# A one-core attention and feed-forward kernel: first steps reordered, state tokens in three passes, second block's low parts and final stores moved

## The chip, the core and the metric

The kernel runs on one core of a Trainium2 chip. The metric is device time in microseconds (us), the median of several executions. Five engines work side by side, each through its own queue in order: TensorE (PE in the profile; its weight loads are PEld), VectorE (DVE), ScalarE (ACT), GpSimd (POOL) and SyncE (SP), which here only issues DMAs. ACT can issue DMAs too. A matmul multiplies a stationary operand (`lhsT`) by a moving operand of up to 512 columns and adds the result up in PSUM.

## The reference

For 8 batches of 512 tokens (`x`) and 32 state tokens (`state`), 8 heads of 64 columns each:

```python
a      = softmax(x @ state^T / 8);  xread = a @ state        # x reads the state
a2     = softmax(state @ x^T / 8);  sread = a2 @ x           # the state reads x
y      = concat(xread, sread)                # 8 x 544 tokens x 512 columns
yn     = (y - mean(y)) / sqrt(var(y) + 1e-6) * g_ln
x2     = y + relu(yn @ w_ch1) @ w_ch2        # feed-forward, 512 -> 2048 -> 512
gate   = sigmoid(causal 5-tap convolution of x2 along the tokens, per column)
out    = (gate * (x2 @ w_val)) @ w_out
```

Inputs `x` and `state` are float32, the weights arrive in 64-bit form and are decoded on the chip.

## The kernel before, in words

**Number formats.** A plain f32 matmul shows as two MATMUL instructions in the profile. Most products use three passes of the faster f32r form instead: each operand is split into a high part (rounded to f32r, by ACT) and a low part (the rest, by a subtraction on DVE or POOL), and `mm3` (L76) issues high times low, low times high, high times high. `split_sb` (L72) makes the two parts.

**Weights.** `w_ch1` and `w_ch2` are 16 tiles each of 128 x 512 (512 KB raw). `tile_stages` (L484) decodes one tile: `decode_a` (two ACT operations), `decode_b` (four DVE operations, L455, L457, L458, L462), and for most `w_ch2` tiles a split. The raw tiles of `w_ch1` share four buffers (`raw`), so the load of tile 4 waits until tile 0 is decoded. The order in which tiles are taken is the list `order` (L730): `w_ch2` tiles 0 and 1, `w_ch1` tile 4, and so on. `share` (L895) says how many are emitted at each block.

**Feed-forward.** Hidden units go in 16 blocks of 128 (`f`), four blocks to a quarter `q`. For ordinary tokens layer 1 is not done on the tokens: `m_steps` (L132) multiplies the 32 state rows of each head by the quarter's weights, `colsum` (L152) supplies the column sums that subtract the mean, and a block is then `h = m^T aT` with `aT` the attention weights. In the first segment (batch 0, `f` 0 to 3) `m`, `aT` and `w_ch2` are plain f32 (L559, L595); all else is three-pass with `ahl`, the split of `aT`. `colsum(q)` for `q` > 0 is four pairs of matmuls into `parts`, an ACT copy (L161), one product over the copy (L163) and another copy.

`segment` (L536) runs the blocks: at each `f` the PE gets `h(f)`, then the second layer of `f - 1` (12 matmuls into four accumulators), and one step of a background generator `bg`. Segments: batch 0 blocks 0 to 7, batch 1 blocks 0 to 7, batch 0 and 1 blocks 8 to 15, batches 2 to 7 whole, and last all 256 state tokens together (`b == B`). For these, layer 1 is the plain product `w1^T xn` of L565, four pairs of 256-column matmuls a block, then ReLU (L580, ACT), its low part (L582, DVE) and layer 2.

**First steps.** Before segment 0 the program lists by hand what PE, ACT and DVE do (L863 to L887): state coefficients, decode of `w_ch1` tiles 0 to 3 (`st`), the scores of batch 0, its softmax, the column sums of quarter 0, `m` of quarter 0, and the decode of `w_ch2` tile 0 (`w20`). `fill` puts warm-up matmuls into PE's queue. `first()` (L779) is the background of segment 0: x1 of batch 0 in two groups, its mean and variance, the attention of batch 1, and the state read of batch 0.

**Second block.** After the state segment, each batch `i` is loaded back from DRAM (`x2d`, into one of two `big` buffers), split (`split_x2`, L637: ACT high, POOL low, for batch 0 DVE low), gated (`gate_x2`, L649: ACT, four DVE taps L658, ACT sigmoid L670), multiplied by `w_val` (`val_steps`, L681) and by `w_out` (`out_steps`, L697). The split and gate of batch 0 and the decode of `w_out` are background of the state segment; those of batch 1 come beside `val_steps(0)`. `w_out`'s raw tiles are loaded into the buffers of `w_ch1` tiles once those are free.

**What sets the order.** Only PE's queue (and in the first steps ACT's and DVE's) follows the program. For the other engines a planner places each operation by priority (`at_prio`; a smaller number goes first, `HLEAD` = 4000 is four blocks ahead) on its own estimated clock, and each engine then keeps that order. `behind(ins, mark)` forbids an operation from being placed ahead of the last one that set the mark (`"dve"`, `"act"`, `"q1"`, `"s"`). Loads go to SP's queue in the planned order; `load_state(0)` and `load_x(0)` go to ACT's.

**Final stores.** The state tokens' output rows are stored as two DMAs of 256 KB (L709), each 4 batches x 32 rows.

Of the kernel before, what the change touches and what calls it, by code (L numbers as in the profile page):

```python
# [9 lines left out]
F32 = mybir.dt.float32  # L10
# [34 lines left out]
def tile_kernel(ctx: ExitStack, tc: tile.TileContext, xT, xk, stT, sn, w1, w2, wval, wout, convw, gln, ident, out):  # L45
# [105 lines left out]

    def colsum(q, between=lambda k: None):  # L152
        if q:
            parts = at_ps([P, S])
            for k in range(KT):
                nc.tensor.matmul(
                    parts[32 * k:32 * k + 32, :], lhsT=g_sb[:, k].to_broadcast([P, 32]), rhs=w1s[4 * q + k],
                    start=True, stop=True,
                )
            t = t2([P, S])  # L160
            nc.scalar.copy(t, parts)  # L161
            cp = at_ps([P, S])
            nc.tensor.matmul(cp, lhsT=part.to_broadcast([P, P]), rhs=t, start=True, stop=True)  # L163
            nc.scalar.copy(cs[:, q], cp)
            cs_done.add(q)
            return
        cp = at_ps([P, S])
        for k in range(KT):
            nc.tensor.matmul(
                cp, lhsT=g_sb[:, k].to_broadcast([P, P]), rhs=w1s[4 * q + k], start=k == 0, stop=k == KT - 1  # L170
            )
            between(k)
        marks["act"] = nc.scalar.copy(cs[:, q], cp)
        cs_done.add(q)
# [39 lines left out]
    def softmax1_split(b):  # L214
        ahls[b] = ahl = sb([P, 2, 2, S], F32R, "ahl")
        for u in range(2):
            split_sb(ahl[:, u, 0], ahl[:, u, 1], aTs[b][:, u], nc.vector)

# [115 lines left out]
    def x1_steps(b):  # L334
        _, sn_raw, _, sbhl = coef[b]
        ahl, aT = ahls[b], aTs[b]
# [12 lines left out]
        mu = at_ps([P, S])  # L349
        for u in range(2):  # L350
            h, l = sbhl[:, 0, u].to_broadcast([P, P]), sbhl[:, 1, u].to_broadcast([P, P])
            mm3(mu, h, l, ahl[:, u, 0], ahl[:, u, 1], u == 0, u == 1)
        sqs = []
        for k in range(KT):
            xc = t2([P, S])
            nc.vector.tensor_tensor(xc, x1[:, k], mu, op=ALU.add)
            nc.scalar.activation(xc, xc, AF.Square)
# [48 lines left out]
    def sread_block_steps():  # L406
# [7 lines left out]
        xc = sb([P, KT, NTS], F32, "big")  # L414
        xn = sb([P, KT, NTS], F32, "ahl")
        for k in range(KT):
            nc.vector.tensor_tensor(xc[:, k], xs[:, k], mu, op=ALU.add)
        yield
        for k in range(KT):
            nc.scalar.activation(xn[:, k], xc[:, k], AF.Copy, scale=g_sb[:, k])  # L420
        xns[B] = xn
# [25 lines left out]
    def decode_a(r, c):  # L447
        a = nc.scalar.activation(c, r[:, :, 1].bitcast(F32), AF.Abs)
        behind(a, "act")
        a = nc.scalar.activation(r[:, :, 0].bitcast(I32), r[:, :, 0], AF.Copy, scale=2.0 ** -29)  # L450
        behind(a, "act")

    def decode_b(r, c):
# [30 lines left out]
    def tile_stages(kind, j):  # L484
        if kind == "1":
# [5 lines left out]
            def second():  # L491
                a = decode_b(r, c)
                if j == 2 * KT - 1:
                    marks["q1"] = a

            return lambda: decode_a(r, c), second, lambda: None
        if kind == "s":
# [9 lines left out]
            return split, lambda: None, lambda: None  # L507
        if j < QF:
            if j % 2 == 0:
# [3 lines left out]
            return lambda: decode_a(r, c), lambda: decode_b(r, c), lambda: None  # L513
        r, c = raws["2", j], sb([P, DM], F32, "c")
# [18 lines left out]
    cs_done = set()  # L533
    clock = [BASE]

    def segment(b, f0, f1, n, nxt, bg):  # L536
        accs = {}
        for f in range(f0, f1):
# [7 lines left out]
            fresh = b < B and unit is not None and unit[1] not in cs_done  # L546
            if b < B and unit is not None and f % QF == 1 and not fresh:
                at_prio(base - 1500)
                m_steps(*unit)
            at_prio(base - HLEAD)  # L550
            if f == 1 and 1 < b < B:
                x1_group(b)
            at_prio(base)
            h = ps(ps_mm, "mm", [P, n])
            if b < B:
                m = ms[b, q]
                for u in range(2):
# [4 lines left out]
                    mm3(h, m[:, u, 0, cols], m[:, u, 1, cols], ahl[:, u, 0], ahl[:, u, 1], u == 0, u == 1)  # L562
            else:
                for k in range(KT):
                    nc.tensor.matmul(  # L565
                        h, lhsT=w1s[4 * q + k][:, cols], rhs=xns[b][:, k], start=k == 0, stop=k == KT - 1
                    )
            if fresh and f % QF == 3:
                at_prio(base - 1500)
                colsum(unit[1])  # L570
                m_steps(*unit)
# [65 lines left out]
    def split_x2(i, k):  # L637
# [4 lines left out]
        behind(nc.scalar.activation(hi, src, AF.Copy), "act")  # L642
        if i:
            nc.gpsimd.tensor_tensor(lo, src, hi.bitcast(F32), op=ALU.subtract)  # L644
# [27 lines left out]
    def x2_steps(i):  # L672
        if i > B:
            return
        for k in range(KT):
            split_x2(i, k)
            yield
            gate_x2(i, k)
            yield

    def val_steps(i):  # L681
# [4 lines left out]
        for e in range(KT):  # L686
# [5 lines left out]
            hl = sb([P, 2, n], F32R, f"w2_{8 + 4 * (i % 2) + e}")  # L692
            split_sb(hl[:, 0], hl[:, 1], gt[:, e], nc.vector)
            gvs[i].append(hl)
            yield

    def out_steps(i):  # L697
        n = ntok(i)
        hls = gvs.pop(i)
        for t in range(n // P):  # L700
# [7 lines left out]
            if i == B:  # L708
                nc.sync.dma_start(out=out[4 * t:4 * t + 4, S:, :], in_=ob[:, t % 2])  # L709
            elif t % 2:  # L710
# [31 lines left out]
    load_state(0, nc.scalar)  # L742
    load_x(0, nc.scalar)
    load_tile("1", 1)
    nc.sync.dma_start(out=g_sb.rearrange("p k o -> p (k o)"), in_=gln)
    for j in range(2, KT):
# [32 lines left out]
    def first():  # L779
# [4 lines left out]
        state_coefs(1)  # L784
        yield
        next(x1)
        yield
# [5 lines left out]
        yield  # L793
        next(att1)
        yield
        for _ in x1:
            pass
        softmax2_turn(0)
        yield
        sread(0)  # L800
# [62 lines left out]
    with tc.manual_schedule(engines={mybir.EngineType.PE, mybir.EngineType.Activation, mybir.EngineType.DVE}):  # L863
# [21 lines left out]
        fill(6)  # L885
        w20[1]()
        slots[0] = decode_slots(order[1:])  # L887
    with tc.manual_schedule(engines={mybir.EngineType.PE}):
# [3 lines left out]
        next(slots[0])  # L892
        at_prio(BASE - 5000)
        softmax1_split(0)
        share[0] = iter([1, 2, 2, 5, 2, 1, 1, 0] + [1, 2] * 4 + [1] * 8)  # L895
# [67 lines left out]
```

## Time and profile before

| | us |
|---|---|
| three runs | 944.11, 946.27, 946.20 |
| median | 946.2 |
| the profiled execution | 944.02 |
| its span, first to last instruction | 942.2 |
| PE busy | 911.7 (97%) |
| DVE busy | 563.9 (60%) |
| ACT busy | 367.4 (39%) |
| POOL busy | 193.1 (20%) |

The mean granted TensorE clock is 0.992 of full speed. Busy time of PE counts the warm-up matmuls too, and a matmul's recorded length is longer than the distance to the next, since they are pipelined. What a stage could give is therefore read from distances between starts and from idle time, stage by stage.

### The profile page before, as it was taken

The page shows a single profiled execution, that of the slowest core. Times are in us where ns is not written, and L with a number is a line of the kernel's source. Part 1 is how long each engine was busy: PE and PEld are TensorE (multiplying, and loading weights), DVE is VectorE, ACT ScalarE, POOL GpSimd, SP SyncE. Part 2 cuts the span into 40 slices and gives each one's busy share as a digit, 9 for nine tenths or more (in the row PEclk, how much of TensorE's full clock was granted, in tenths as well). Part 3 has the DMA queues.
Part 4 walks back from the last instruction along what each step waited for, and adds up shares of the span by engine and source line. Part 5 has one row for each costly group of instructions (what it writes and reads, how often), then busy time and mean ns, then how long its engine had stood idle before and what let it go on. Part 6 is the DMA issues. An engine that isn't in the chain of part 4 may idle for free.

```text
span 942.2 us, 12810 instructions
## 1 busy us (share of the span) xinstructions
PE 911.7 (97%) x5087; PEld 687.9 (73%) x5088; DVE 563.9 (60%) x972; ACT 367.4 (39%) x672; POOL 193.1 (20%) x167
## 2 busy tenths in 40 slices
PE   7979999999999999999999999999999989999996
PEld 2327666777777777777777777777888878888884
DVE  6887997575357472453436336242138899988830
ACT  4646654233144332332314233232125454655521
POOL 0000000012114521412411241142102243232100
PEclk9989999999999999999999999999999999999999
DMA  9832220022103111111100110110021212321112
GB/s 364 325 114 93 71 71 1 1 93 96 41 8 118 46 48 48 48 48 49 48 21 25 48 45 1 27 46 18 27 90 46 90 45 90 129 96 62 51 67 67
DMA packets 26548, 66.45 MB, mean 71 GB/s; under 512 B 10744, under 2 KB 12920, under 8 KB 22392
## 3 DMA queue, kind: packets, MB, share of 16 engines
q1 hardware_dynamic: 26056, 64.45, 19.2%
q10 hardware_dynamic: 432, 1.18, 0.3%
q8 instruction: 40, 0.66, 0.3%
q14 instruction: 20, 0.16, 0.1%
HBM read 47.80 MB, written 17.83 MB: 70 GB/s over the span
## 4 chain that ended last, share of the span: by engine, by line
PE 79%; DVE 14%; DMA 2%; ACT 2%; issue 1%; SPq 0%; ACTq 0%; DVEq 0%
PE acc L77 14%; PE acc L79 14%; PE acc L78 13%; PE mm L77 8%; PE mm L79 7%; PE mm L78 7%; PE at L138 3%; DVE ahl L658 3%; PE at L77 2%; PE at L79 2%; PE at L78 2%; PE mm L565 1%; PE acc L595 1%; DVE w L458 1%; DVE hid L582 1%
## 5 line engine op out<-in xcount | busy, mean ns | idle before, releaser
L582 DVE SCALAR_TENSOR_TENSOR hid<-mm,hid 128x512 fp32r<-128x512 f32 (+1 forms) x140 | 92.2, 658 | 223.6 <-ACT hid L580 223.4
L77 PE MATMUL acc<-hid,w 128*128 128x512 f32 (+1 forms) x560 | 215.7, 385 | 2.3 <-DVE hid L582 1.2
L79 PE MATMUL acc<-hid,w 128*128 128x512 f32 (+1 forms) x560 | 211.5, 378 | 0.0
L78 PE MATMUL acc<-hid,w 128*128 128x512 f32 (+1 forms) x560 | 211.2, 377 | 0.0
L580 ACT ACTIVATE hid<-mm 128x512 fp32r<-128x512 f32 (+2 forms) x144 | 82.4, 572 | 246.8 <-PE mm L79 226.8
L77 PEld LDWEIGHTS acc<-hid,w 128*128 128x128 f32 x560 | 105.3, 188 | 25.4 <-DVE hid L582 2.2
L79 PEld LDWEIGHTS acc<-hid,w 128*128 128x128 f32 x560 | 105.3, 188 | 20.0
L78 PEld LDWEIGHTS acc<-hid,w 128*128 128x128 f32 x560 | 105.4, 188 | 19.4
L74 POOL TENSOR_TENSOR m<-mb,m 128x512 fp32r<-128x512 f32 x48 | 65.5, 1379 | 202.0 <-ACT m L73 202.0
L77 PE MATMUL mm<-ahl,m 128*128 128x512 f32 x248 | 102.3, 413 | 0.0
L658 DVE SCALAR_TENSOR_TENSOR ahl<-big,cw,ahl 128x509 f32<-128x509 f32 (+3 forms) x128 | 99.4, 830 | 4.1 <-ACT ahl L656 3.7
L78 PE MATMUL mm<-ahl,m 128*128 128x512 f32 x248 | 96.8, 390 | 0.2 <-DVE m L74 0.2
L79 PE MATMUL mm<-ahl,m 128*128 128x512 f32 x248 | 96.9, 391 | 0.0
L77 PEld LDWEIGHTS mm<-ahl,m 128*128 128x128 f32 x248 | 46.5, 188 | 38.0 <-issue 30.0
L73 ACT ACTIVATE m<-mb 128x512 fp32r<-128x512 f32 x62 | 39.1, 630 | 89.8 <-DVE mb L144 89.7
L644 POOL TENSOR_TENSOR w<-big,w 128x512 fp32r<-128x512 f32 x28 | 44.2, 1605 | 82.0 <-ACT w L642 82.0
L144 DVE SCALAR_TENSOR_TENSOR mb<-cs,sbn,at 128x512 f32<-128x512 f32 x62 | 43.5, 742 | 28.3 <-PE at L138 28.3
L77 PE MATMUL acc<-w,raw 128*128 128x512 f32 (+1 forms) x144 | 54.6, 379 | 2.5 <-DVE ahl L691 2.5
L78 PE MATMUL acc<-w,raw 128*128 128x512 f32 (+1 forms) x144 | 54.4, 378 | 0.0
L79 PE MATMUL acc<-w,raw 128*128 128x512 f32 (+1 forms) x144 | 54.3, 377 | 0.0
L79 PEld LDWEIGHTS mm<-ahl,m 128*128 128x128 f32 x248 | 46.5, 188 | 10.1
L78 PEld LDWEIGHTS mm<-ahl,m 128*128 128x128 f32 x248 | 46.7, 188 | 8.5 <-DVE m L74 0.5
(172 smaller groups left out, 1353.3 us busy)
## 6 DMA issues: line engine op xcount, KB each, us to landing
raw<-in_w SPq DMA_DIRECT2D x16, 512.0 KB, 4.7
w<-in_w SPq DMA_DIRECT2D x16, 512.0 KB, 9.8
big<-in_xk SPq DMA_DIRECT2D x8, 1024.0 KB, 4.9
x2d<-x SPq DMA_DIRECT2D x8, 1024.0 KB, 3.8
big<-x2d SPq DMA_DIRECT2D x8, 1024.0 KB, 4.9
out<-hid SPq DMA_DIRECT2D x16, 512.0 KB, 2.8
big<-in_xT SPq DMA_DIRECT2D x7, 1024.0 KB, 4.8
raw<-in_wval SPq DMA_DIRECT2D x4, 512.0 KB, 3.5
```

The source lines that it names most:

```text
L73: nc.scalar.activation(hi, src, AF.Copy)
L74: eng.tensor_tensor(lo, src, hi.bitcast(F32), op=ALU.subtract)
L77: nc.tensor.matmul(acc, lhsT=wh, rhs=xl, start=first, stop=False)
L78: nc.tensor.matmul(acc, lhsT=wl, rhs=xh, start=False, stop=False)
L79: nc.tensor.matmul(acc, lhsT=wh, rhs=xh, start=False, stop=last)
L138: nc.tensor.matmul(mp[u][32 * p:32 * p + 32, :], lhsT=stg[r, p, :], rhs=w1s[4 * q + p][r], start=True, stop=True)
L144: a = nc.vector.scalar_tensor_tensor(mb, cs[:, q], sbn[:, u], mp[u], op0=ALU.mult, op1=ALU.add)
L458: a = nc.vector.tensor_scalar(h[:, :, 0, 1], h[:, :, 1, 1], 0x8000, 0x4000, op0=ALU.bitwise_and, op1=ALU.bitwise_or)
L580: marks["act"] = nc.scalar.activation(hid[:, 0], h, AF.Relu)
L582: marks["dve"] = nc.vector.scalar_tensor_tensor(hid[:, 1], h, 0.0, hid[:, 0].bitcast(F32), op0=ALU.max, op1=ALU.subtract)
L644: nc.gpsimd.tensor_tensor(lo, src, hi.bitcast(F32), op=ALU.subtract)
L658: t = nc.vector.scalar_tensor_tensor(g[:, j:], x[:, :n - j], cw_sb[:, k, PAD - j:TAPS - j], g[:, j:], op0=ALU.mult, op1=ALU.add)
```

## The change

In the first steps: `load_x(0)` goes to SP behind `w_ch1` tiles 0 and 1, and the load of `g_ln` to ACT's queue; the split of `aT` of batch 0 is made later, behind the decode of quarter 1 (mark `"q1"`, set by `w_ch1` tile 7); decodes emitted later are kept behind `w_ch2` tile 0 and behind `w_ch1` tile 7 on DVE and ACT; the mean of x1 of batch 0 comes one step later, its DVE part at a higher priority; the parts of `colsum(2)` and `colsum(3)` are issued ahead of the block's `h`; `m_steps(1, 0)` comes one block later; `softmax2_turn(0)` one step earlier.

For the state tokens: `xn` and the `w_ch1` columns of two blocks at a time are split into high and low (`split_w1`), and layer 1 is `mm3`.

In the second block: the low parts of batch 1 are made on DVE, its four splits before its four gates; `val_steps` sets the mark `"dve"`. Each final store becomes four stores of 32 rows (64 KB), alternately on SP and ACT.

```diff
     def softmax1_split(b):
...
-            split_sb(ahl[:, u, 0], ahl[:, u, 1], aTs[b][:, u], nc.vector)
+            nc.scalar.activation(ahl[:, u, 0], aTs[b][:, u], AF.Copy)
+            a = nc.vector.tensor_tensor(ahl[:, u, 1], aTs[b][:, u], ahl[:, u, 0].bitcast(F32), op=ALU.subtract)
+            if b == 0:
+                behind(a, "q1")
...
+                    marks["q1"] = marks["dve"] = a
...
+    def split_w1(i):
+        hl = sb([P, 2, KT, 2 * P], F32R, "m")
+        q, c = i // 2, slice((i % 2) * 2 * P, (i % 2 + 1) * 2 * P)
+        for j in range(2):
+            w = w1s[2 * q + j, "pair"][:, :, c]
+            split_sb(hl[:, 0, 2 * j:2 * j + 2], hl[:, 1, 2 * j:2 * j + 2], w, nc.vector)
+        w1hl[i] = hl
...
+            if fresh and f % QF == 3 and unit[1] > 1:
+                at_prio(base - 1500)
+                colsum_parts(unit[1])
             at_prio(base - HLEAD)
+            if b == B and f % 2 == 0:
+                if f == 0:
+                    split_w1(0)
+                if f + 2 < f1:
+                    split_w1(f // 2 + 1)
...
-                    nc.tensor.matmul(
-                        h, lhsT=w1s[4 * q + k][:, cols], rhs=xns[b][:, k], start=k == 0, stop=k == KT - 1
-                    )
+                    mm3(h, w[:, 0, k, wc], w[:, 1, k, wc], xn[:, 0, k], xn[:, 1, k], k == 0, k == KT - 1)
...
-        if i:
+        if i > 1:
             nc.gpsimd.tensor_tensor(lo, src, hi.bitcast(F32), op=ALU.subtract)
...
             if i == B:
-                nc.sync.dma_start(out=out[4 * t:4 * t + 4, S:, :], in_=ob[:, t % 2])
+                for j in range(4):
+                    eng = nc.scalar if j % 2 else nc.sync
+                    eng.dma_start(out=out[4 * t + j, S:, :], in_=ob[32 * j:32 * j + 32, t % 2])
...
     load_state(0, nc.scalar)
-    load_x(0, nc.scalar)
     load_tile("1", 1)
-    nc.sync.dma_start(out=g_sb.rearrange("p k o -> p (k o)"), in_=gln)
+    load_x(0)
+    nc.scalar.dma_start(out=g_sb.rearrange("p k o -> p (k o)"), in_=gln)
...
         colsum(0, lambda k: fill((10, 10, 6, 0)[k]))
         m_steps(0, 0)
         fill(6)
-        w20[1]()
+        marks["dve"] = w20[1]()
...
-        at_prio(BASE - 5000)
-        softmax1_split(0)
```

## Rows read from the trace of the kernel before

**Rows 1.** Busy time by stage: length, us (x) of PE, PEld, DVE, ACT, POOL; clock, DMA, GB/s.
```profile
28.00:61.00 33.00, 25.85 (x80) 8.35 (x78) 27.61 (x56) 19.46 (x36) 0.00 (x0) 0.90 0.60 223
61.00:100.00 39.00, 37.27 (x256) 24.08 (x250) 32.34 (x66) 20.52 (x38) 1.02 (x1) 1.00 0.26 85
100.00:156.00 56.00, 53.15 (x314) 38.32 (x312) 52.51 (x105) 33.16 (x61) 1.40 (x1) 1.00 0.19 60
156.00:689.00 533.00, 531.91 (x3173) 405.31 (x3173) 247.89 (x431) 165.91 (x303) 134.91 (x118) 1.00 0.12 42
689.00:742.50 53.50, 52.30 (x327) 47.79 (x326) 35.98 (x60) 21.59 (x42) 7.41 (x9) 1.00 0.20 72
742.50:770.00 27.50, 25.02 (x115) 20.30 (x114) 26.82 (x34) 12.91 (x23) 13.30 (x8) 1.00 0.15 54
```

**Rows 2.** Timeline of PE, segment 0: start, us, what, [idle before, releaser].
```profile
34.76 3.67 PE L595 MATMUL acc<-hid,w 128*128 128x512 f32 x8 [2.15 <-DVE w L462]
...
54.25 1.91 PE L156 MATMUL at<-w,g 128*32 128x512 f32 x2 [3.84 <-DVE w L462]
```

**Rows 3.** Busy time of the stretch behind PE's longest wait (columns as in rows 1).
```profile
54.10:60.90 6.80, 5.97 (x20) 1.08 (x20) 5.71 (x11) 2.22 (x4) 0.00 (x0) 0.50 0.50 154
```

**Rows 4.** Timeline of DVE, segment 0.
```profile
28.13 0.75 DVE L455 TENSOR_SCALAR w<-w 128x512 f32<-128x512 f32 x2
...
42.69 0.43 DVE L455 TENSOR_SCALAR w<-w 128x512 f32<-128x512 f32 x1 [2.29 <-ACT w L448]
43.15 0.43 DVE L457 TENSOR_SCALAR w<-w 128x512 uint32<-128x512 uint32 x1
43.49 0.75 DVE L458 TENSOR_SCALAR raw<-raw 128x512 uint16<-128x512 uint16 x1
46.22 2.48 DVE L356 TENSOR_TENSOR t<-x,at 128x512 f32<-128x512 f32 x4 [1.99 <-PE at L79]
...
53.51 0.69 DVE L462 CUSTOM_DVE_ANT_0 w<-raw,w 128x1024 uint16<-128x1024 uint16 x1
```

**Rows 5.** Timelines of SP and ACT: raw tiles of quarter 1.
```profile
29.91 10.28 SPq L433 DMA_DIRECT2D raw<-in_w  x4
...
43.12 0.67 ACT L448 ACTIVATE w<-raw 128x512 f32<-128x512 f32 x1
```

**Rows 6.** Timeline of DVE, its first wait.
```profile
6.47 0.28 DVE L121 TENSOR_REDUCE sbn<-sn_raw 128x2 f32<-128x128 f32 x1 [5.22 <-DMA sn_raw<-in_sn]
```

**Rows 7.** Timeline of PE, column sums of quarter 2.
```profile
132.33 1.12 PE L163 MATMUL at<-t,part 128*128 128x512 f32 x2 [1.30 <-ACT t L161]
```

**Rows 8.** Timeline of PE, one block of the state tokens.
```profile
695.98 1.89 PE L565 MATMUL mm<-ahl,w 128*128 128x256 f32 x8
...
697.82 0.28 PE L78 MATMUL acc<-hid,w 128*128 128x256 f32 x1
697.94 0.28 PE L79 MATMUL acc<-hid,w 128*128 128x256 f32 x1
...
699.13 1.89 PE L565 MATMUL mm<-ahl,w 128*128 128x256 f32 x8
```

**Rows 9.** Groups by line and form, state segment: count | busy, mean ns | idle before.
```profile
L646 DVE TENSOR_TENSOR w<-big,w 128x512 fp32r<-128x512 f32 x4 | 3.0, 756 | 0.1
```

**Rows 10.** Timeline of SP, loads of the second block.
```profile
739.41 30.03 SPq L635 DMA_DIRECT2D big<-x2d  x3
```

**Rows 11.** Timeline of PE, behind the state segment.
```profile
761.81 0.50 PE L77 MATMUL acc<-w,raw 128*128 128x512 f32 x1 [1.48 <-DVE ahl L691]
...
765.85 0.50 PE L77 MATMUL acc<-w,raw 128*128 128x512 f32 x1 [1.01 <-DVE ahl L691]
```

**Rows 12.** SP's waits: us in total, times, longest.
```profile
SPq L959 <- DMA out<-hid: 6.8, 1, 6.8
```

**Rows 13.** Busy time of the end, behind the last matmuls (columns as in rows 1).
```profile
932.20:941.00 8.80, 0.95 (x5) 0.45 (x3) 0.00 (x0) 0.59 (x1) 0.00 (x0) 0.84 0.21 60
```

**Rows 14.** DMA issues, ordinary stores: count, KB each, median us to landing.
```profile
out<-hid SPq DMA_DIRECT2D x16, 512.0 KB, 2.8
```

More of the change, by code (lines that the diff above doesn't have):

```diff
@@ L150, in m_steps, with colsum_parts @@
                 split_sb(m[:, u, 0], m[:, u, 1], mb, nc.vector if b < 2 else nc.gpsimd)
-    def colsum(q, between=lambda k: None):
+    def colsum_parts(q):
         if q:
@@ L159, in colsum @@
                 )
-            t = t2([P, S])
+            cs_part[q] = t = t2([P, S])
             nc.scalar.copy(t, parts)
+    cs_part = {}
+    def colsum(q, between=lambda k: None):
+        if q:
+            t = cs_part[q]
             cp = at_ps([P, S])
@@ L335, in x1_steps @@
         _, sn_raw, _, sbhl = coef[b]
-        ahl, aT = ahls[b], aTs[b]
+        aT = aTs[b]
         x1 = sb([P, KT, S], F32, "x1")
@@ L348, in x1_steps @@
             yield
-        mu = at_ps([P, S])
+        mu, ahl = at_ps([P, S]), ahls[b]
         for u in range(2):
@@ L355, in x1_steps @@
             xc = t2([P, S])
+            p = tc.cur_priority
+            at_prio(p - HLEAD)
             nc.vector.tensor_tensor(xc, x1[:, k], mu, op=ALU.add)
+            at_prio(p)
             nc.scalar.activation(xc, xc, AF.Square)
@@ L414, in sread_block_steps @@
         xc = sb([P, KT, NTS], F32, "big")
-        xn = sb([P, KT, NTS], F32, "ahl")
+        xn = sb([P, 2, KT, NTS], F32R, "ahl")
         for k in range(KT):
@@ L419, in sread_block_steps @@
         for k in range(KT):
-            nc.scalar.activation(xn[:, k], xc[:, k], AF.Copy, scale=g_sb[:, k])
+            nc.scalar.activation(xn[:, 0, k], xc[:, k], AF.Copy, scale=g_sb[:, k])
+            nc.vector.scalar_tensor_tensor(
+                xn[:, 1, k], xc[:, k], g_sb[:, k], xn[:, 0, k].bitcast(F32), op0=ALU.mult, op1=ALU.subtract
+            )
         xns[B] = xn
@@ L451, in decode_a @@
         behind(a, "act")
+        return a
     def decode_b(r, c):
@@ L493, in second, with first @@
                 if j == 2 * KT - 1:
-                    marks["q1"] = a
-            return lambda: decode_a(r, c), second, lambda: None
+                    marks["q1"] = marks["dve"] = a
+            def first():
+                a = decode_a(r, c)
+                if j == 2 * KT - 1:
+                    marks["act"] = a
+            return first, second, lambda: None
         if kind == "s":
@@ L508, in tile_stages, with add @@
         if j < QF:
+            def add():
+                return decode_b(r, c)
             if j % 2 == 0:
@@ L512, in tile_stages @@
             r = raws["2", j]
-            return lambda: decode_a(r, c), lambda: decode_b(r, c), lambda: None
+            return lambda: decode_a(r, c), add, lambda: None
         r, c = raws["2", j], sb([P, DM], F32, "c")
@@ L534, in tile_kernel @@
     clock = [BASE]
+    w1hl = {}
+    def split_w1(i):
[5 more added lines that the diff above has]
+        w1hl[i] = hl
     def segment(b, f0, f1, n, nxt, bg):
@@ L546, in segment @@
             fresh = b < B and unit is not None and unit[1] not in cs_done
-            if b < B and unit is not None and f % QF == 1 and not fresh:
+            if b < B and unit is not None and f % QF == (2 if unit == (1, 0) else 1) and not fresh:
                 at_prio(base - 1500)
                 m_steps(*unit)
+            if fresh and f % QF == 3 and unit[1] > 1:
+                at_prio(base - 1500)
+                colsum_parts(unit[1])
             at_prio(base - HLEAD)
+            if b == B and f % 2 == 0:
[3 more added lines that the diff above has]
+                    split_w1(f // 2 + 1)
             if f == 1 and 1 < b < B:
@@ L563, in segment @@
             else:
+                wc = slice((f % 2) * P, (f % 2 + 1) * P)
+                w, xn = w1hl[f // 2], xns[b]
                 for k in range(KT):
-                    nc.tensor.matmul(
-                        h, lhsT=w1s[4 * q + k][:, cols], rhs=xns[b][:, k], start=k == 0, stop=k == KT - 1
-                    )
+                    mm3(h, w[:, 0, k, wc], w[:, 1, k, wc], xn[:, 0, k], xn[:, 1, k], k == 0, k == KT - 1)
             if fresh and f % QF == 3:
                 at_prio(base - 1500)
+                if unit[1] == 1:
+                    colsum_parts(1)
                 colsum(unit[1])
@@ L677, in x2_steps @@
             yield
-            gate_x2(i, k)
-            yield
+            if i != 1:
+                gate_x2(i, k)
+                yield
+        if i == 1:
+            for k in range(KT):
+                gate_x2(i, k)
+                yield
     def val_steps(i):
@@ L692, in val_steps @@
             hl = sb([P, 2, n], F32R, f"w2_{8 + 4 * (i % 2) + e}")
-            split_sb(hl[:, 0], hl[:, 1], gt[:, e], nc.vector)
+            nc.scalar.activation(hl[:, 0], gt[:, e], AF.Copy)
+            a = nc.vector.tensor_tensor(hl[:, 1], gt[:, e], hl[:, 0].bitcast(F32), op=ALU.subtract)
+            marks["dve"] = a
             gvs[i].append(hl)
@@ L785, in first @@
         yield
+        yield
+        softmax1_split(0)
         next(x1)
@@ L794, in first @@
         next(att1)
+        softmax2_turn(0)
         yield
@@ L797, in first @@
             pass
-        softmax2_turn(0)
-        yield
         sread(0)
```

## The prediction

> **What bounds the kernel now.** I read the busy time by stage first [rows 1]. From 156 us to the state tokens at 689 us PE is busy 531.9 of 533 us and the change adds only four low parts there, so this stage stays. What is left is four places: the first 156 us, the state segment, the stretch behind it, and the end. In 28 to 61 us PE is busy 25.9 of 33.0 us and its clock averages 0.90; DVE is busy 27.6. In 61 to 156 us both are near full (PE 90.4, DVE 84.9 of 95 us), so time won by one must be won by the other too. In the state segment PE is busy 52.3 of 53.5 us and DVE 36.0. From 742.5 to 770 us it is the reverse: DVE 26.8 of 27.5, PE 25.0. Then the timelines, to see what PE waits for: in segment 0 chiefly twice for the last operation (L462) of a weight tile's decode, 2.15 and 3.84 us [rows 2], and after the second of these its clock is granted at 0.50, the level of 1.2 GHz, for 6.8 us [rows 3].
>
> **First steps.** Removed: DVE's delays ahead of two decodes. A tile costs DVE 0.43 + 0.43 + 0.75 + 0.69 = 2.3 us [rows 4]. Before, tile 0 of `w_ch2` begins at 28.13 us [rows 4] but is mixed with other decodes and the split of `aT` (two subtractions), and PE starts on it at 34.76, 2.15 us after its last matmul [rows 2]; kept together it ends near 30.5, before PE is free at 32.6: the 2.15 us are won. Next come seven tiles, 7 x 2.3 = 16.1 us, so `w_ch1` tile 7 can be decoded at 46.6 instead of 54.2 [rows 4]. Two things stand in its way. Its raw load is among those issued from 29.91 us on, and ACT takes it at 43.12 [rows 5]; ACT then needs 1.3 us and DVE 2.3, giving 46.7, much the same. And DVE idles 2.29 us before tile 6, for ACT, then 1.99 us for the mean's matmuls, with tile 6 half done [rows 4]; the new order puts the mean behind tile 7, so the second goes. PE reaches the column sums at about 44 us and waits 1 to 3 us instead of 3.84, so I take the half clock to go as well. It costs half of the 5.97 us in rows 3, 3.0 us. PE's side could give 2.15 + 3.84 + 3.0 = 9.0 us.
>
> DVE's side caps this. No DVE work goes away, it is only put behind (the split, the mean's four subtractions and three sums, two tiles of `w_ch2`). From 28 to 100 us DVE idles 72 - 59.95 = 12.1 us [rows 1]; what must stay is some 1 to 2 us for tile 6's load, and waits for PE results (scores, the hidden block) that I put at 4. So 12.1 - 6 = 6: I take **-6.0**, ends -9.0 and +2 (the marks forbid filling DVE's wait for tile 6 or 7 with other work, one wait of 2.29 us more).
>
> `x` behind tile 1 on SP: DVE's first work waits 5.22 us for `sn_raw`, not for `x` [rows 6], and that load keeps its queue and place. `g_ln` comes later on ACT's queue, but PE's column sums want it only after two tiles' decode on DVE, 4.6 us. The same bytes are loaded in nearly the same order, so 0, ends +1 and -1. `m_steps(1, 0)` and `softmax2_turn(0)` move by a block among PE work with nothing idle behind it: 0; if `m` of batch 1 came late, its four DVE operations (2.7 us) would be the price.
>
> Column sums of quarters 2 and 3: PE waits 1.30 us for ACT's copy [rows 7], the longer of two such waits, 2.1 us together; with the parts ahead of `h` its six matmuls cover the copy. The copy is queued on ACT with hidden blocks and decodes behind it, which it holds no longer than now. But DVE is busy 52.5 of 56 us there [rows 1], so I take half, **-1.0**, ends 0 and -2.1.
>
> **State tokens.** Now a block is 8 plain MATMULs from 695.98 to about 697.5 and 12 three-pass ones to 699.13, a period of 3.15 us; inside the three-pass run the starts are 0.12 us apart [rows 8]. Three passes for both layers are 24 x 0.12 = 2.87 us. 16 x 0.28 = 4.5 us. Added: 8 `split_w1`, each two ACT and two DVE operations of 128x512. The like of it on DVE (L646) takes 0.756 us in this segment [rows 9], so 16 cost 12.1 us; four come before 689 us, where DVE is busy 248 of 533 us [rows 1]. The segment then holds 36.0 + 9.1 = 45.1 us of DVE work in 53.5 - 4.5 = 49.0 us. It fits, but barely. Two helpers: `w_out`'s loads are freed by the split rather than by the matmul, some blocks earlier, so its decode fills DVE's empty start; and the split is made up to four blocks ahead. The low parts of `xn` (four operations) hide where DVE is mostly idle. If the hidden block's low part comes late by a DVE operation now and then, PE waits. I allow 1.0 us: **-3.5**, ends -4.5 and +5 (half of the 9.1 us of new DVE work finds no place, and nothing is won).
>
> **Second block.** PE waits 1.48 and 1.01 us for L691 [rows 11], queued on DVE behind the gates of batch 1. Four subtractions (3.0 us) move to DVE, but the gates now come behind the splits and behind the first products, and PE needs gates(1) only for the third product, some 20 us later. **-2.5**, ends 0 and -2.5, a late load apart (rival C). Cover: the load of batch 1 is issued when batch 0's gates end, 739.41 [rows 10], 3 us before the state segment does, and PE's first product, 48 matmuls of 512 columns, twice 0.12 us each, gives it 11.5 us more; if the gates end more than a few us later, PE waits for the difference.
>
> **Final stores.** SP waits 6.8 us for the last store [rows 12], in a stretch where the 16 DMA engines are busy 0.21 of the time, as 3.4 engines would be, at 60 GB/s [rows 13]; a store of 512 KB on the same queue lands 2.8 us after issue [rows 14]. Four stores of 64 KB on two queues should each land like that store at most. The last is issued one DMA issue (about 0.4 us) later than now, so the wait is 2.8 + 0.4 = 3.2 at most, and as the transfer is an eighth of it, near 2.4: 6.8 - 2.4 = **-4.4**, ends 0 and -4.9.
> The Trainium skill, "DMA: Bandwidth & Descriptors", section "Why a DMA increments its semaphore by 16 and not by 1", says that a DMA uses the largest number of engines up to 16 that divides the slowest dimension of both sides: 4 for the old store of 4 batches, 16 for 32 rows. The trace agrees for the old store (3.4 engines on average); of 32 rows it shows nothing.
> The same page's "Rules for kernel authors" speaks against the change: a transfer split over partitions shares the same engines, and one transfer of all partitions is better. By that rule alone the term would be 0, as in rival D.
>
> **Sum.** -6.0 - 1.0 - 3.5 - 2.5 - 4.4 = -17.4, against the profiled execution: span 942.2, its time 944.0, so 926.6. That execution lies at the low end of the runs shown (944.1, 946.2, 946.3), 2.2 under their median; I forecast 927.5 for the median.
>
> **Rivals.** (A) The forecast, 0.55. (B) The first steps give nothing, since DVE's work and the raw loads set the end of this part: 927.5 + 7 = 934.5. For it: DVE is 94% busy in 100 to 156 us; against: its 12.1 us of idle time before. 0.17. (C) DVE becomes the bound of the state segment and batch 1's load is late: the -3.5 and -2.5 go and 3 us come on top, 936.5. For it: 45.1 of 49.0 us; against: the decode that `w_out`'s earlier loads bring forward. 0.12. (D) The pieces do not spread over more engines: 256 KB at the present rate take what they took, and 6.8 us of wait stay: 932.0. Against: the ordinary store's 2.8 us for twice the bytes. 0.08. (E) Slower: each block of state tokens hands its weights PE to ACT to DVE to PE, since the split's two buffers are freed only by a matmul. If the hand-over lies open in each block, ACT 0.67 [rows 5] and DVE 0.76 us [rows 9], 16 x 1.4 = 22.4 us come on top: 949.9. It decides from 17.4 / 16 = 1.1 us a block. Against: a buffer is free for some five half-blocks (7 us) before it is wanted. 0.05. (F) The planner's own clock, not the marks, sets DVE's order, and old waits come back elsewhere in all places: about 943. 0.03.
>
> **Numbers.** The range of 920 to 938 takes in 926.6 with all terms at their better ends (944.0 - 23.0 = 921.0), B, D and most of C. Faster by over 0.3% (2.8 us, about what this measurement tells from none): A to D, 0.92. Same: F, 0.03. Slower: E, 0.05.
>
> **What would show it.** Right: in segment 0 `w_ch1` tile 7 is decoded by 47 us, no half clock behind it, and batch 1's first block starts 6 us earlier; state blocks 2.9 us apart; no PE wait for L691; SP's last wait under 3 us. Wrong: the column sums of quarter 1 still waiting past 50 us, PE idle before the hidden blocks of the state tokens on DVE's L582 or on the split, or a last wait of 6 us.

## The result, and the profile after

The changed kernel takes 933.91 us (median of 4 runs, 933.0 to 936.34), the one before 945.15 us in the same comparison (944.08 to 946.27): ratio 0.9891, 95% interval 0.9875 to 0.9906. It is faster by 11 us, inside the range, but 6.4 us above the forecast: nearest to rival B (934.5 us). The profiled execution took 934.39 us, its span 932.6 us. Its stages against those of before, from the starts of PE's first matmul of the state tokens (687.42 before, 689.52 after), of its first product of the second block (743.83, 742.45), of its last matmul (932.76, 928.28), and the end:

| | forecast | traces |
|---|---|---|
| up to the state tokens (first steps and column sums) | -7.0 | +2.1 |
| state segment (56.4, now 52.9 us) | -3.5 | -3.5 |
| second block, first product to the start of the last matmul (188.9, now 185.8 us) | -2.5 | -3.1 |
| behind that start (9.4, now 4.3 us) | -4.4 | -5.1 |
| sum, spans | -17.4 | -9.6 |

Three rows came out within 0.7 us. The first falls short by 9.1 us, more than the whole shortfall of 7.8. The stages of [rows 1] after the change (length, busy time of PE, weight loads, DVE, ACT, POOL, then granted clock, DMA share, GB/s), and below them the stretch that answers to [rows 3]:

```profile
28.00:61.00 33.00, 27.60 (x83) 9.11 (x82) 26.85 (x53) 18.98 (x35) 0.00 (x0) 0.84 0.60 225
61.00:100.00 39.00, 35.19 (x240) 22.86 (x239) 30.13 (x61) 20.70 (x38) 1.34 (x1) 0.96 0.25 85
100.00:156.00 56.00, 54.41 (x318) 39.52 (x318) 53.49 (x107) 32.39 (x59) 3.35 (x1) 1.00 0.19 60
689.00:742.50 53.50, 51.43 (x413) 50.27 (x412) 44.64 (x76) 27.96 (x55) 8.78 (x9) 1.00 0.22 79
742.50:770.00 27.50, 27.50 (x123) 22.77 (x123) 23.76 (x36) 14.26 (x24) 6.16 (x4) 1.00 0.11 39
...
50.14:58.50 8.36, 7.68 (x22) 1.70 (x23) 8.12 (x16) 2.54 (x5) 0.00 (x0) 0.50 0.39 125
```

From 28 to 100 us DVE idles 72 - 56.98 = 15.0 us, more than the 12.1 of before; the clock is lower (0.84 and 0.96), and the half clock (0.50, the level of 1.2 GHz) lasts at least 8.4 us instead of 6.8. From 742.5 us PE is busy throughout: the waits of [rows 11] are gone. PE's timeline of the changed kernel, at the places of [rows 2], [rows 7] and [rows 8]:

```profile
32.74 3.60 PE L639 MATMUL acc<-hid,w 128*128 128x512 f32 x8
...
44.35 1.06 PE L156 MATMUL at<-w,g 128*32 128x512 f32 x6
50.14 1.92 PE L156 MATMUL at<-w,g 128*32 128x512 f32 x2 [4.72 <-DVE w L478]
...
137.25 1.09 PE L138 MATMUL at<-w,stg 64*32 64x512 f32 x14 [0.46 <-ACT cs L170]
...
710.95 0.39 PE L77 MATMUL acc<-hid,w 128*128 128x256 f32 x1 [0.33 <-DVE hid L626]
715.83 0.39 PE L77 MATMUL acc<-hid,w 128*128 128x256 f32 x1 [1.74 <-DVE hid L626]
```

The first wait of [rows 2] is gone: the second layer starts at 32.74 instead of 34.76 us. Of the two waits of [rows 7] 0.46 us is left, for a copy that comes later (L170). In the state segment PE waits 0.33 and 1.74 us for the hidden block's low part (L626). PE comes to the last two parts of the column sums at 45.4 us and then waits 4.72 us, longer than the 3.84 of before. It waits for DVE, and DVE (its timeline first) for ACT (below it), which answers to [rows 4] and [rows 5]:

```profile
43.27 0.69 DVE L478 CUSTOM_DVE_ANT_0 w<-raw,w 128x1024 uint16<-128x1024 uint16 x1
47.82 0.43 DVE L471 TENSOR_SCALAR w<-w 128x512 f32<-128x512 f32 x1 [3.86 <-ACT w L463]
```

```profile
41.55 0.69 ACT L465 ACTIVATE raw<-raw 128x512 int32<-128x512 uint32 x1
44.46 0.60 ACT L624 ACTIVATE hid<-mm 128x512 f32<-128x512 f32 x1 [2.22 <-PE mm L601]
44.95 0.66 ACT L463 ACTIVATE c<-w 128x512 f32<-128x512 f32 x1
...
46.60 0.64 ACT L465 ACTIVATE w<-w 128x512 int32<-128x512 uint32 x1
47.15 0.64 ACT L463 ACTIVATE w<-raw 128x512 f32<-128x512 f32 x1
```

ACT ends tile 6 at 42.2 us and then stands 2.22 us before hidden block 3, whose matmuls PE ends at 44.4 us. Behind that relu it decodes tiles 4 and 5 of `w_ch2`, and only at 47.15 us tile 7 of `w_ch1`, 4 us later than the 43.12 of [rows 5]. The code says why: each hidden block's relu overwrites `marks["act"]`. Tile 7's decode sets that mark, the relu of block 3 replaces it, and the decodes of tiles 4 and 5 are kept behind the relu alone. Nothing keeps the relu or these decodes behind tile 7, and the planner put them ahead. So the change keeps later decodes behind tile 7 on DVE, but not on ACT.

The end: SP's last waits (in total, times, longest), which answer to [rows 12], and the stretch behind the last copy, which answers to [rows 13]:

```profile
SPq L1011 <- DMA out<-hid: 1.4, 2, 1.2
```

```profile
929.30:931.50 2.20, 0.00 (x0) 0.00 (x0) 0.00 (x0) 0.00 (x0) 0.00 (x0) 1.00 0.46 119
```

### The profile page after: what moved, and what is told of

Same layout as the page of the kernel before. It is cut to its first block, busy times and chain, and to the rows that moved or that the text cites. A ratio compares the mean times of both kernels' runs of the same rounds, so it can differ in the third digit from the quotient of the medians.

```text
span 932.6 us, 12963 instructions
## 1 busy us (share of the span) xinstructions
PE 909.9 (98%) x5152; PEld 688.8 (74%) x5152; DVE 579.5 (62%) x996; ACT 375.7 (40%) x688; POOL 191.8 (21%) x163
## 4 chain that ended last, share of the span: by engine, by line
PE 90%; DVE 5%; DMA 2%; ACT 1%; issue 1%; SPq 0%; ACTq 0%; DVEq 0%
PE acc L77 16%; PE acc L79 15%; PE acc L78 15%; PE mm L77 9%; PE mm L79 8%; PE mm L78 8%; PE at L138 4%; PE at L77 2%; PE at L78 2%; PE at L79 2%; PE mm L913 1%; PE acc L639 1%; PE at L385 1%; DMA big<-in_xT 1%; PE mm L601 1%; PE at L276 1%
## 5 line engine op out<-in xcount | busy, mean ns | idle before, releaser
L626 DVE SCALAR_TENSOR_TENSOR hid<-mm,hid 128x512 fp32r<-128x512 f32 (+1 forms) x140 | 92.2, 659 | 211.7 <-ACT hid L624 211.6
L77 PE MATMUL mm<-ahl,m 128*128 128x512 f32 (+1 forms) x312 | 121.2, 388 | 0.0
L78 PE MATMUL mm<-ahl,m 128*128 128x512 f32 (+1 forms) x312 | 115.3, 370 | 0.0
L79 PE MATMUL mm<-ahl,m 128*128 128x512 f32 (+1 forms) x312 | 115.3, 370 | 0.0
L702 DVE SCALAR_TENSOR_TENSOR ahl<-big,cw,ahl 128x511 f32<-128x511 f32 (+3 forms) x128 | 103.3, 851 | 0.4
L77 PEld LDWEIGHTS mm<-ahl,m 128*128 128x128 f32 x312 | 59.0, 189 | 40.3 <-issue 32.3
L79 PEld LDWEIGHTS mm<-ahl,m 128*128 128x128 f32 x312 | 59.0, 189 | 10.2
L78 PEld LDWEIGHTS mm<-ahl,m 128*128 128x128 f32 x312 | 59.2, 190 | 8.5 <-DVE m L74 0.5
L688 POOL TENSOR_TENSOR w<-big,w 128x512 fp32r<-128x512 f32 x24 | 38.4, 1629 | 93.6 <-ACT w L686 77.0
```

The source lines that it names most:

```text
L77: nc.tensor.matmul(acc, lhsT=wh, rhs=xl, start=first, stop=False)
L78: nc.tensor.matmul(acc, lhsT=wl, rhs=xh, start=False, stop=False)
L79: nc.tensor.matmul(acc, lhsT=wh, rhs=xh, start=False, stop=last)
L626: marks["dve"] = nc.vector.scalar_tensor_tensor(hid[:, 1], h, 0.0, hid[:, 0].bitcast(F32), op0=ALU.max, op1=ALU.subtract)
L702: t = nc.vector.scalar_tensor_tensor(g[:, j:], x[:, :n - j], cw_sb[:, k, PAD - j:TAPS - j], g[:, j:], op0=ALU.mult, op1=ALU.add)
```

## Experiments

All times are medians; "mended" is the kernel of experiment 2, 925.57 us.

**1. All but the first steps.** The kernel before with the new state tokens, second block and stores; the hunks of `tile_stages`, `softmax1_split`, `x1_steps`, `first`, `colsum`, the place of `m_steps(1, 0)`, the mark of `w20` and the loads are left out. Against the changed kernel:

```diff
-            cs_part[q] = t = t2([P, S])
+            t = t2([P, S])
...
-        marks["dve"] = w20[1]()
+        w20[1]()
...
```

> The kernel before with the changes of the state tokens, the second block and the final stores alone: the first steps and the column sums stay as they were. The trace of the changed kernel reaches the state segment 2.1 us later than the one before (689.52 against 687.42 us), so theory 1, the new first steps cost time: about 2 us less than the changed kernel, 932 us. Theory 2, the forecast was right and the shift is chance of one execution: 7 us more than the changed kernel, 941 us. Theory 3, the first steps move nothing: 934 us, within 1 us of the changed kernel.

933.18 us (932.19 to 935.0), ratio 0.9869 (0.9851 to 0.9888). Theory 3: the first steps move nothing. The state tokens start at 690.09 us here and at 687.42 in the trace of before, with the same first steps; with the changed ones at 689.52, 687.78 and 686.77 us (the changed kernel, experiments 3 and 4). So one trace says no more than some 3 us on this part, the +2.1 of my table lies within that, and the averages (688.8 and 688.0) differ by 0.8 us. Part of the spread is the clock: in the three traces with the changed first steps PE waits the same at the column sums (4.72, 4.72 and 4.73 us), but over 28 to 61 us the granted clock is 0.84 in the first and 0.90 in the other two.

**2. ACT's order mended.**

```diff
-            marks["act"] = nc.scalar.activation(hid[:, 0], h, AF.Relu)
+            a = nc.scalar.activation(hid[:, 0], h, AF.Relu)
+            if b == 0 and f == 3:
+                behind(a, "act")
+            marks["act"] = a
```

> The changed kernel with one order added: ACT's relu of hidden block 3 (L624) stands behind ACT's half of the decode of w_ch1 tile 7, and so do the decodes of w_ch2 tiles 4 and 5 that follow that relu. Theory 1, ACT's order is what makes PE wait 4.72 us at 45.4 us: ACT takes tile 7 at 42.2 instead of 47.15 us, DVE ends it at 46.3 instead of 50.1, PE waits about 1 us and keeps its clock; 4 to 6 us less, 928 to 930 us. Theory 2, the raw tile lands late: ACT waits for the DMA and takes tile 7 at 45 us or later; under 1 us less. Theory 3, DVE sets the end of this part: tile 7 is done at 46.3 us and PE's wait goes, but batch 1's first block starts no earlier than 99 us and the time stays at 933 to 934 us.

925.57 us (924.52 to 927.17), ratio 0.9794 (0.9777 to 0.9811): 8.3 us less than the changed kernel, more than theory 1 gave. ACT, DVE and PE in its timelines:

```profile
42.02 0.69 ACT L463 ACTIVATE w<-raw 128x512 f32<-128x512 f32 x1
...
45.14 0.69 DVE L478 CUSTOM_DVE_ANT_0 w<-raw,w 128x1024 uint16<-128x1024 uint16 x1
...
45.89 1.04 PE L156 MATMUL at<-w,g 128*32 128x512 f32 x2 [0.56 <-DVE w L478]
...
68.62 2.62 PE L138 MATMUL at<-w,stg 64*32 64x512 f32 x16 [2.14 <-ACT t L245]
...
80.77 1.10 PE L276 MATMUL at<-big,t 128*32 128x64 f32 x64 [1.47 <-ACT t L264]
```

ACT takes tile 7 at 42.02 us with no wait, so the raw tile had landed; DVE ends it at 45.8; PE waits 0.56 us, and the clock stays at 1.00 from 45 to 61 us. DVE's idle time from 28 to 100 us falls to 7.6 us. The state tokens start at 681.49 us, and at 680.13 to 682.39 in the four other kernels that change nothing else ahead of them (experiments 7 and 9 to 11).

**3 and 4. What makes the store pieces fast.** On the changed kernel, two pieces of two batches on two queues, and four pieces on one queue.

```diff
-                for j in range(4):
+                for j in range(2):
                     eng = nc.scalar if j % 2 else nc.sync
-                    eng.dma_start(out=out[4 * t + j, S:, :], in_=ob[32 * j:32 * j + 32, t % 2])
+                    eng.dma_start(out=out[4 * t + 2 * j:4 * t + 2 * j + 2, S:, :], in_=ob[64 * j:64 * j + 64, t % 2])
```

> The changed kernel with each final store in two pieces of two batches each (64 rows of the tile), one on SP's and one on ACT's queue, instead of four of one batch each. Theory 1, a store uses as many DMA engines as its outer dimension allows (the batches), so two stores of two batches use four engines like the one store of before, and 256 KB take about what they took: the last wait is 6 to 7 us again, 937 to 939 us. Theory 2, what counts is that the bytes are split over two queues: two pieces of 128 KB land about as soon as four of 64 KB, 934 us, at most 1 us more.

```diff
-                    eng = nc.scalar if j % 2 else nc.sync
-                    eng.dma_start(out=out[4 * t + j, S:, :], in_=ob[32 * j:32 * j + 32, t % 2])
+                    nc.sync.dma_start(out=out[4 * t + j, S:, :], in_=ob[32 * j:32 * j + 32, t % 2])
```

> The changed kernel with the four pieces of each final store all on SP's queue. Theory 1, the pieces' shape makes them fast and the second queue saves only two issues of 0.35 us behind the last copy: 0.7 us more, 934 to 935 us. Theory 2, one queue serves one store after the other: four landings in a row of 1.5 us or more, 3 us more, 937 us.

Two pieces: 942.69 us, ratio 0.998 (0.9968 to 0.9991), nearly all of the change's gain lost, and slower than either theory gave. From the end of ACT's last copy to the end of the span it takes 12.6 us, against 8.4 with the one store of before and 3.3 with four pieces. The stretch behind that copy, and SP's last waits:

```profile
931.00:939.00 8.00, 0.00 (x0) 0.00 (x0) 0.00 (x0) 0.00 (x0) 0.00 (x0) 0.51 0.13 49
```

```profile
SPq L1011 <- DMA out<-hid: 11.0, 2, 9.8
```

A share of 0.13 is 2 of 16 engines, at 49 GB/s: not 2 + 2. The Trainium skill, "DMA: Bandwidth & Descriptors", section "Why a DMA increments its semaphore by 16 and not by 1", says that a DMA uses as many engines, up to 16, as divide the slowest dimension, and that SP's and ACT's DMAs take the lowest-numbered ones; two stores of two batches then share two engines, and the trace agrees. I had read the first half only. With four pieces of 32 rows the rule gives 16 engines; their share behind the last copy is 0.46 over 2.2 us, so the trace shows only that more than four take part.

One queue: 935.65 us (932.5 to 937.54), ratio 0.9897 (0.9879 to 0.9915), not to be told from the changed kernel; from the last copy to the end it takes 3.9 us instead of 3.3. Theory 1: the shape of the pieces is what counts, the second queue saves issues, 0.6 us.

**5 and 6. PE's other waits in segment 0.** On the mended kernel: batch 1's first m products a block later, and the state read a step later.

```diff
-            if b < B and unit is not None and f % QF == (2 if unit == (1, 0) else 1) and not fresh:
+            if b < B and unit is not None and f % QF == (3 if unit == (1, 0) else 1) and not fresh:
```

> The changed kernel with ACT's order mended (925.6 us), and batch 1's first m products (L138) put one hidden block later, at block 7 of segment 0. There PE waits 2.14 us at 66.5 us, because these products want the two PSUM buffers in which batch 1's scores lie until ACT's exponentials are done at 69.2 us. Theory 1, a block later the buffers are free and PE has the second layer to do: the wait and the slow matmuls behind it go, 2 to 3 us less, 922.5 to 923.5 us. Theory 2, the wait comes back at the transposes (L262) that follow and want the same two buffers, which DVE frees only behind its softmax work: no change, 925 to 926.5 us.

```diff
         for _ in x1:
             pass
-        sread(0)
         yield
...
         x1 = x1_steps(1)
         next(x1)
+        sread(0)
         yield
```

> The changed kernel with ACT's order mended (925.6 us), and the state read of batch 0 (L276) put a step later, into the next segment, as it stood a step behind its transposes before the change. There PE waits 1.47 us at 79.3 us for ACT's copy of the transposes (L264). Theory 1, that wait is on the path: 1.5 us less, 924 us. Theory 2, DVE sets the end of this part, so PE waits elsewhere by as much: 925.6 us, within 0.5 us.

927.26 us (ratio 0.9817, 0.9799 to 0.9835) and 928.82 us (0.9825, 0.9806 to 0.9844): neither gains, as theory 2 had it, but both take longer than it gave, 1.7 and 3.2 us more than mended. The waits come back (PE's timeline of 5, then of 6):

```profile
77.54 1.63 PE L138 MATMUL at<-w,stg 64*32 64x512 f32 x14 [3.90 <-ACT t L264]
```

```profile
81.80 0.50 PE L77 MATMUL mm<-ahl,m 128*128 128x512 f32 x1 [1.12 <-DVE ahl L224]
...
89.30 1.10 PE L276 MATMUL at<-big,t 128*32 128x64 f32 x64 [0.67 <-ACT x L356]
93.55 1.09 PE L138 MATMUL at<-w,stg 64*32 64x512 f32 x14 [2.18 <-DVE t L280]
```

The two PSUM buffers pass from the scores to the transposes to the m products; whoever comes last waits for the copy out of them.

**7. The weight split's low parts on POOL** (mended kernel).

```diff
-            split_sb(hl[:, 0, 2 * j:2 * j + 2], hl[:, 1, 2 * j:2 * j + 2], w, nc.vector)
+            split_sb(hl[:, 0, 2 * j:2 * j + 2], hl[:, 1, 2 * j:2 * j + 2], w, nc.gpsimd)
```

> The changed kernel with ACT's order mended (925.6 us), and the low parts of the state tokens' weight split on POOL instead of DVE, 16 subtractions of 128x512. Theory 1, DVE's queue is what makes PE wait 0.30 and 1.74 us for the hidden block's low part (L629) in the state segment: with 12 us of DVE work gone both waits go, 2 us less, 923.5 us. Theory 2, POOL's 1.3 us for such a subtraction, or DVE's slower operations beside it, makes the split late: PE waits for the split instead, 926 to 930 us.

929.07 us, ratio 0.9828 (0.9811 to 0.9844): the state segment takes 55.4 instead of 52.9 us, with PE waiting 0.33, 1.21, 1.54 and 1.14 us. It waits for DVE's L629, the hidden block's low part, and not for the split: of theory 2 the slower DVE came, the late split did not. DVE's groups from 690 to 742 us (line, shape, count | busy us, mean ns | idle before), first here, then mended:

```profile
L705 DVE SCALAR_TENSOR_TENSOR ahl<-big,cw,ahl 128x511 f32<-128x511 f32 (+3 forms) x16 | 15.9, 997 | 1.8 <-ACT ahl L703 1.6
L474 DVE TENSOR_SCALAR w<-w 128x512 uint16<-128x512 uint16 x4 | 5.2, 1299 | 0.0
L471 DVE TENSOR_SCALAR c<-c 128x512 f32<-128x512 f32 x4 | 3.5, 875 | 2.6 <-ACT c L463 2.5
```

```profile
L705 DVE SCALAR_TENSOR_TENSOR ahl<-big,cw,ahl 128x511 f32<-128x511 f32 (+3 forms) x16 | 13.0, 812 | 0.2
L74 DVE TENSOR_TENSOR m<-w,m 128x512 fp32r<-128x512 f32 x12 | 7.7, 682 | 0.1
L474 DVE TENSOR_SCALAR w<-w 128x512 uint16<-128x512 uint16 x4 | 4.1, 1024 | 1.8 <-ACT w L465 1.7
L471 DVE TENSOR_SCALAR c<-c 128x512 f32<-128x512 f32 x4 | 1.7, 434 | 0.1
```

12 subtractions (7.7 us) left DVE, and it is as busy as before: 44.2 us in this segment against 44.1. What stays takes longer beside POOL.

**8. Column sums' parts back behind `h`** (mended kernel).

```diff
-            if fresh and f % QF == 3 and unit[1] > 1:
-                at_prio(base - 1500)
-                colsum_parts(unit[1])
...
-                if unit[1] == 1:
-                    colsum_parts(1)
+                colsum_parts(unit[1])
                 colsum(unit[1])
```

> The changed kernel with ACT's order mended (925.6 us), and the parts of the column sums of quarters 2 and 3 put back behind the hidden block's matmuls. Theory 1, their place ahead of those matmuls hides ACT's copy: the two waits of before, 1.30 and 0.77 us, come back where 0.44 us is left now, 1.6 us more, 927.2 us. Theory 2, DVE sets the end of this part: 925.6 us, within 0.5 us.

929.12 us, ratio 0.9833 (0.9813 to 0.9852): theory 1 and more. Both waits are back where 0.44 us was left:

```profile
129.52 1.12 PE L169 MATMUL at<-t,part 128*128 128x512 f32 x2 [1.30 <-ACT t L161]
...
152.47 1.12 PE L169 MATMUL at<-t,part 128*128 128x512 f32 x2 [1.02 <-ACT t L161]
```

That is 1.9 us. The state tokens start 3.4 us later than in the mended trace. The other 1.5 us are lost where nothing was edited: PE starts its products at L276 at 80.72 us, behind the same wait of 1.47 us as mended (80.77), but the m products that follow at 93.01 instead of 91.51. Behind that wait the clock was granted at 0.50 here and at 1.00 in the mended trace (first here, then mended):

```profile
80.70:84.00 3.30, 3.28 (x67) 2.86 (x68) 3.30 (x8) 1.13 (x2) 1.68 (x1) 0.50 0.20 25
```

```profile
80.70:84.00 3.30, 3.23 (x74) 2.76 (x75) 3.30 (x8) 1.18 (x3) 1.72 (x1) 1.00 0.32 67
```

So this part is no price of the edit; why the clock fell in one execution and not in the other stays open.

**9 to 11. One term undone at a time** (mended kernel): plain layer 1 for the state tokens; the low parts of batch 1 on POOL and its gates between its splits; one store per block.

```diff
-                    mm3(h, w[:, 0, k, wc], w[:, 1, k, wc], xn[:, 0, k], xn[:, 1, k], k == 0, k == KT - 1)
+                    nc.tensor.matmul(
+                        h, lhsT=w1s[4 * q + k][:, cols], rhs=xns[b][:, k], start=k == 0, stop=k == KT - 1
+                    )
...
```

> The changed kernel with ACT's order mended (925.6 us), and layer 1 of the state tokens in plain float32 again, as before the change. Theory 1, the three passes are worth the 3.5 us by which the state segment became shorter: 3.5 us more, 929 us. Theory 2, part of that is given back behind the segment, since DVE has 12 us less to do in it without the weight split, and the stretch behind it is bound by DVE: 1.5 to 2.5 us more, 927 to 928 us.

```diff
-        if i > 1:
+        if i:
             nc.gpsimd.tensor_tensor(lo, src, hi.bitcast(F32), op=ALU.subtract)
...
```

> The changed kernel with ACT's order mended (925.6 us), and the second block's edits undone: the low parts of batch 1 on POOL, its gates between its splits. Theory 1, as forecast, PE waits again 1.5 and 1.0 us for those low parts: 2.5 to 3.1 us more, 928 to 929 us. Theory 2, with the shorter state segment the waits lie elsewhere and PE loses more, since the splits come later against PE: 4 to 6 us more, 930 to 932 us.

```diff
-                for j in range(4):
-                    eng = nc.scalar if j % 2 else nc.sync
-                    eng.dma_start(out=out[4 * t + j, S:, :], in_=ob[32 * j:32 * j + 32, t % 2])
+                nc.sync.dma_start(out=out[4 * t:4 * t + 4, S:, :], in_=ob[:, t % 2])
```

> The changed kernel with ACT's order mended (925.6 us), and the final stores as before the change, one of four batches each on SP's queue. Theory 1, the 5.1 us by which the end behind the last copy became shorter come back: 930.7 us. Theory 2, as with two pieces, a store's time hangs on the others that are in flight on the same engines, and it is not the same at each run: 4 to 8 us more.

928.55 us (ratio 0.9822, 0.9808 to 0.9837), 927.80 us (0.9811, 0.9796 to 0.9827) and 931.29 us (0.9842, 0.9827 to 0.9858): 3.0, 2.2 and 5.7 us more than mended. By the ratios it is 2.6, 1.6 and 4.5 us, since the kernel before took 946.38 us beside these runs and 944.55 beside the mended one. The traces say it more sharply. Without the three passes the state segment takes 56.4 us again, +3.5, and the stretch behind it is not changed (185.8 us): theory 1. Without the second block's edits that stretch takes 187.7 us, +1.8. PE waits again for L738, which stands behind the gates of batch 1 in DVE's queue, 0.23 us and then:

```profile
753.80 0.50 PE L77 MATMUL acc<-w,raw 128*128 128x512 f32 x1 [1.03 <-DVE ahl L738]
```

That is less than theory 1 gave, and less than the 3.1 us from before to after. With plain state tokens and the old second block it took 188.9 us, so some 1.2 us of those 3.1 are won by either of the two edits. Without the pieces the end behind the last copy takes 8.4 us, +5.1: theory 1.

**12. Both remaining waits by order** (mended kernel): m products two blocks earlier, `w_out`'s decode a block later.

```diff
-            if b < B and unit is not None and f % QF == (2 if unit == (1, 0) else 1) and not fresh:
+            if b < B and unit is not None and f % QF == (0 if unit == (1, 0) else 1) and not fresh:
...
+        yield
         yield from prep_weights(wout, wo, [f"w1_{k}" for k in range(KT)])
```

> The changed kernel with ACT's order mended (925.6 us), batch 1's first m products (L138) put two hidden blocks earlier, at block 4 of segment 0, ahead of batch 1's scores; and w_out's decode put one block later in the state segment. Theory 1, both waits of PE are matters of order: 2.14 us at 66.5 us and 1.74 us at 706 us go, 921.8 to 923 us. Theory 2, DVE is the bound in the first of these places (busy 33.9 of 35 us from 45 to 80 us): its four operations for m, 2.7 us, now stand ahead of a hidden block's low part, and PE waits for that instead; and the decode's wait only moves: 925 to 926.5 us.

935.05 us, ratio 0.9879 (0.986 to 0.9898): 9.5 us more than mended (8.0 by the ratios), beyond both theories. PE's timeline at the two places, and the stretches behind them:

```profile
59.52 1.96 PE L138 MATMUL at<-w,stg 64*32 64x512 f32 x14 [2.75 <-DVE t L367]
...
752.91 0.50 PE L77 MATMUL acc<-w,raw 128*128 128x512 f32 x1 [2.39 <-DVE w L693]
754.60 0.50 PE L77 MATMUL acc<-w,raw 128*128 128x512 f32 x1 [0.72 <-DVE w L693]
```

```profile
59.52:63.00 3.48, 3.48 (x18) 1.52 (x19) 2.69 (x5) 1.25 (x4) 0.00 (x0) 0.50 0.02 5
...
756.00:770.00 14.00, 14.00 (x58) 11.44 (x57) 13.46 (x22) 7.00 (x12) 0.00 (x0) 0.90 0.06 11
```

The earlier products want the PSUM buffer of the mean, which DVE's L367 frees: 2.75 us, and half a clock behind it; the state tokens start 3.8 us later than in the mended trace. The later decode shortens the state segment by 0.7 us, but batch 0's gates come later: SP starts batch 1's load from `x2d` 1.5 us before PE's first product instead of 4.3, and PE waits 3.4 us for batch 1's splits (L693; 0.29 us before the two shown). Behind that the clock is low again, and the stretch takes 191.7 us, +5.9.

## Why the prediction was right or wrong

The time lies inside the range because the range was drawn wide enough to take in rival B; the forecast's largest term came to about nothing.

**First steps, -6.0: the step that failed.** It said that tile 7's raw load is taken by ACT "at 43.12" and that DVE ends it at 46.7. The sign that I had named for it came: no decode by 47 us, but the column sums still waiting at 50 us. Yet the rest of that step held: the first wait went (-2.0 us), the new order on DVE had tile 6 ready at 43.96, and the load had landed. But 43.12 was a row of before, and ACT's queue is laid out anew with the change; I checked what DVE's marks order and not what ACT's leave free. With one order added (experiment 2) DVE ends at 45.8, PE waits 0.56 us, the half clock goes, and the state tokens start at 681.5 us on average: 7.3 us ahead of the old first steps' 688.8, against -6.0 and -1.0 forecast. Which of the other edits of the first steps bring this gain was not taken apart. The cap by DVE's idle time also came out near: 7.6 us stay, of 12.1, where I had put 6.

**Column sums, -1.0.** Undersized: moving them back costs 1.9 us of waits (experiment 8). I had taken half for DVE's sake.

**State tokens, -3.5.** Right in size and make-up. A three-pass matmul starts every 0.12 us and blocks are 2.88 us apart, as PE's timeline of the changed kernel shows:

```profile
697.50 0.28 PE L77 MATMUL mm<-ahl,m 128*128 128x256 f32 x1
697.62 0.28 PE L78 MATMUL mm<-ahl,m 128*128 128x256 f32 x1
...
700.38 0.28 PE L77 MATMUL mm<-ahl,m 128*128 128x256 f32 x1
```

PE's busy time in the segment falls from 55.2 to 50.9 us (-4.3, against -4.5). Its two waits for the hidden block's low part take 2.07 us; before there were two as well, 0.26 and 0.95 us, so 0.9 us are lost, against 1.0 allowed. Undone alone it costs 3.5 us (experiment 9). Rivals C and E didn't come: DVE is busy 44.6 of 53.5 us, as forecast (45.1), and no block waits for its split.

**Second block, -2.5.** -3.1 in the traces; 1.8 when undone alone. The cover that I named (the load comes when batch 0's gates end) is real: experiment 12 takes it away, and PE waits.

**Final stores, -4.4.** -5.1: the last wait is 1.2 us, I had put 2.4. Rival D is refuted, and experiments 3 and 4 show that the pieces' shape does it. The rule against splitting ("Rules for kernel authors" in the Trainium skill's "DMA: Bandwidth & Descriptors"), whose reason is that both halves already use all 16 engines, doesn't hold for a store whose outer dimension is 4: the trace gives 3.3 us behind the last copy for four pieces, 8.4 for one.

**Rival B** had the right number for another reason: neither DVE's work nor the raw loads set this part, as experiment 2 shows. In kind F came nearest: the planner's own clock, where no mark held it, decided, though on ACT and in one place only.

## What to carry to other kernels

A start time read from a trace holds only while the queue in front of it does: for a step that a planner lays out anew, list on every engine of its chain (here DMA, ACT, DVE, PE) which instructions may now pass it. A mark that later code overwrites no longer orders what is emitted behind that code; keep one for each thing to be ordered. Where engines hand two buffers round, moving one user moved the wait here and won nothing (experiments 5, 6 and 12).

## What the runs showed of the hardware

- Two stores of two batches each, on two queues, took longer together (12.6 us behind the last copy) than one of four (8.4): DMA share 0.13, the same two engines for both.
- Beside POOL's subtractions DVE's L471 took 875 instead of 434 ns and L705 997 instead of 812, so that moving 7.7 us of work off DVE freed none. The Trainium skill's "SBUF — State Buffer", section "SBUF: two separate sides", has an exclusive lock on ports that both engines share; the longer operations agree with it, but no run here shows the lock itself.
- The same wait of PE was followed by either level of its clock. Behind a wait of 2.14 us at 66.5 us the granted clock was 0.50 (1.2 GHz) from 69.3 to 72.6 us in experiment 2 and 1.00 (2.4 GHz) there in experiment 10. Behind one of 1.47 us at 79.3 us it stayed at 1.00 in experiment 2 and was 0.50 from 80.7 to 84.0 us in experiment 8. Such a difference cost 1.5 us, as much as some of the edits are worth.
